# Split score products for eight more slots, a second load queue, a wider value product and a longer weight-splitting plan in an attention-plus-MoE kernel

## The chip, the cores and the metric

The kernel runs on one core of a Trainium2 chip. The metric is device time in microseconds (us); the lower, the better. Three runs of the kernel before took 1076.47, 1074.31 and 1074.10 us, median 1074.31. All matrix work is in fp32: a plain fp32 product takes several passes through TensorE, and the other way that this kernel uses is to write an operand as the sum of two rounded parts (fp32r, high and low) and to add up two or three one-pass products.

## The reference

```python
k_all = np.concatenate([k_g, k_l], axis=2); v_all = np.concatenate([v_g, v_l], axis=2)
out_g = sm(scale * q_g @ k_all.T) @ v_all            # 32 global queries see every key
s_ll = np.where(np.abs(i - j) <= 32, scale * q_l @ k_l.T, -1e9)   # 512 local queries: a band,
out_l = sm(concat[scale * q_l @ k_g.T, s_ll]) @ v_all             # and the 32 global keys
x = concat[out_g, out_l] as (8 * 544, 512)           # 8 batches, 8 heads of 64
h = np.maximum(x @ w_in, 0.0)                        # w_in 512 x 2048
return h * h @ w_out                                 # w_out 2048 x 512
```

## The kernel before, in words

The 128 pieces of attention work (8 batches, 2 halves of 256 local queries, 8 heads) are called slots here, t = 0 to 127. One loop runs over turns t. Turn t does the softmax of slot t, the transposes and the value product of slot t-1, and, 9 turns behind, one eighth (m = t-9) of a block of the MLP: `gemm1` (tiles `h`), relu and square (`r`), `gemm2` (tiles `o`). Block 0, whose x is slots 0 to 7 (`xg`), runs in turns 9 to 16 with plain fp32 weights (`wf`); from m = 8 (turn 17) on the weights are split (`ws`, high and low).

**A slot.** `load_head` brings `raw`: keys (352 columns), queries (256), values (256). `scores` makes `s`. `softmax1` adds the mask on VectorE and takes the maximum (the custom instruction `prob<-s,con`, two a slot), `softmax2` is the exponential on ScalarE, `softmax3` normalises (small `st` instructions, then `prob<-prob,st`). `transposes` brings the probabilities into the PSUM tile `pt`, `pt_split` copies them out (`pts`), `av` makes the value product `xa`, and `x_evac` stores it in `xg` or `x_h`/`x_l`. There are two `prob` tiles and one `pt`, so slot t+2 can't begin its softmax before slot t is transposed.

**Plain slots.** The first 16 slots (`plain`, `NPLAIN`) multiply whole fp32 numbers: scores are one product for each half (two PE records), and the value product has three, of which the first contracts 96 rows. From slot 16 on, `split_head` first makes `hi` and `lo`: a cast on ScalarE (`hi<-raw`), and subtractions on VectorE (`lo`, `hi`). The scores are then two one-pass products for each half. The tiles `hi` and `lo` have two buffers, and `hi` of slot t is also read by `g_scores(t)`, the product with the global queries (`gs`), so `hi` of slot t+2 waits for `g_scores(t)`. That product needs the global queries of four slots: `g_load` loads `qz` in place for plain slots, and loads `qr` and splits it into `qgz` (ScalarE, then VectorE) for the others.

**Weights.** `PLAN` says for each turn, at four places, how many weight passes (`b`) and splits (`s`) are issued. A chunk of weights (`wr`, 32 of them) takes one ScalarE pass and two VectorE passes (`wf`; the letters b count the VectorE passes), and later a cast on ScalarE and a subtraction on VectorE (`ws`). `w_need` issues what a turn needs and the plan hasn't yet issued.

**What sets the order.** From turn 17 on (`FREE`) TensorE, VectorE and ScalarE run in the order of the program text. Before that, a list scheduler at build time orders the instructions of each engine; the chip then runs each engine strictly in that order. So an instruction that waits holds up all that stands behind it on its engine. DMAs are issued by SP, in its own order.

Of the kernel before, what the change touches and what calls it, by code (L numbers as in the profile page):

```python
# [16 lines left out]
P = 128  # L17
# [8 lines left out]
NSTEP = NBLK * 8  # L26
LAG = 9
NPLAIN = 16

PLAN = [",,,b", "b,,,b", "b,,,b", "b,,b,", "b,,b,", "b,,b,", "b,,b,", "b,b,,b", "b,b,,b", "bb,bb,bb,bb", "bb,bb,bb,bb", "bbs,bb,bbs,bbs", "bbs,bbs,bbs,bbs", "bbs,bbs,bbs,bbs", "bbs,bbs,bs,s", "ss,s,s,s", "ss,s,s,s", "s,,s,", "s,,s,", "s,,s,", "s,,s,", "s,,s,", "s,,s,"]  # L30
FREE = (17, 17, 17)
LOOK = 2
SQ = (2, 3, 4, 5, 14, 15)
# [25 lines left out]
def attention_moe(  # L59
# [22 lines left out]
    def plain(t):  # L82
        return t < NPLAIN

    w_bufs = {"free": WCH}

    def w_take(n):
# [2 lines left out]
    def load_head(t):  # L90
        if plain(t):
            w_take(1)
            raw = wp.tile([P, 1024], F32, tag="w", name=f"raw{t}")[:, :PK]
        else:
            raw = p2.tile([P, PK], F32, tag="raw", name=f"raw{t}")
        cuts = (0, QC + KC, PK) if t == 0 else (0, PK)
        for o, e in zip(cuts, cuts[1:]):
            nc.sync.dma_start(raw[:, o:e], pk[t, :, o:e])
        heads[t] = dict(raw=raw)

    load_head(0)
    con = cp.tile([P, P + 4 * WIN], F32, name="con")
    for o, e in ((0, P + 2 * WIN), (P + 2 * WIN, P + 4 * WIN)):
        nc.sync.dma_start(con[:, o:e], consts[:, o:e])
        if o == 0:
            for t in range(1, 4):
                load_head(t)
    ident, masks = con[:, :P], con[:, P:]

    x_h = cp.tile([P, 2, 4, HALF], F32R, name="x_h")  # L110
# [10 lines left out]
    def split_head(t):  # L121

        hd = heads[t]
        raw = hd["raw"]
        if plain(t):
            return
        hi = p2.tile([P, PK], F32R, tag="hi", name=f"hi{t}")
        lo = p2.tile([P, QC + 192], F32R, tag="lo", name=f"lo{t}")
        ac.copy(hi, raw)
        ve.tensor_sub(lo, raw[:, KC : KC + QC + 192], f(hi[:, KC : KC + QC + 192]))  # L130
        ve.tensor_sub(hi[64:, :KC], raw[64:, :KC], f(hi[64:, :KC]))
        ve.tensor_sub(hi[32:64, PK - 64 :], raw[32:64, PK - 64 :], f(hi[32:64, PK - 64 :]))
        hd["hi"], hd["lo"] = hi, lo

    def scores(t):
        hd = heads[t]
        pool, tag = (ps_h, "h") if t < 8 and t % 2 else (ps_a, "s")
        s = pool.tile([P, 2, WIN], F32, tag=tag, name=f"s{t}")
        for u in range(2):
            qs, ks = slice(KC + u * P, KC + u * P + P), slice(128 * u, 128 * u + WIN)  # L140
            if plain(t):
                pe.matmul(s[:, u, :], hd["raw"][:, qs], hd["raw"][:, ks], start=True, stop=True)
            else:
                pe.matmul(s[:, u, :], hd["hi"][:, qs], hd["hi"][:, ks], start=True, stop=False)
                pe.matmul(s[:, u, :], hd["lo"][:, u * P : u * P + P], hd["hi"][:, ks], start=False, stop=True)
        hd["s"] = s

    def scale(t):

        return 0.0625 if plain(t) else 0.125  # L150

    def softmax1(t):
        hd = heads[t]
# [105 lines left out]
    def g_load(t):  # L259

        b, grp = t // 16, (t // 4) % 2

        def cols(z, j):
            return bass.AP(z.tensor, z.offset + 64 * j, [list(z.ap[0]), [256, 2], [160, 2], [1, 32]])

        src = qg[b, grp].rearrange("p (a b) n -> p a b n", a=2)
        if plain(t):
# [12 lines left out]
    def g_scores(t):  # L280
        hd = heads[t]
        h4 = t % 4
        if h4 % 2 == 0:
            state["gs"] = ps_a.tile([P, 416], F32, tag="gs", name=f"gs{t}")
        kk = hd["raw" if plain(t) else "hi"]
        pe.matmul(
            state["gs"][:, :288],
            state["qz"][:, 128 * h4 : 128 * h4 + 128],
# [5 lines left out]
    def g_evac(t):  # L294
        grp, pair = (t // 4) % 2, (t % 4) // 2
        gs = state["gs"]
        early = plain(t)
        parts = ((0, 0, 288),) if (t // 8) % 2 == 0 else ((288, 0, 160), (448, 192, 96))
        parts = [(sg[64 * pair : 64 * pair + 64, grp, d : d + n], slice(o, o + n)) for d, o, n in parts]
        for dst, cols in parts:  # L300
            ac.copy(dst, gs[:64, cols] if early else gs[64:, cols])
        for dst, cols in parts if not early else ():
            ve.tensor_add(dst, gs[:64, cols], dst)

# [16 lines left out]
    def g_soft(t):  # L321
        s = sg[:, (t // 4) % 2, :]
        st = p2.tile([P, 4], F32, tag="gst", name=f"gst{t}")
        ve.tensor_reduce(out=st[:, 0:1], in_=s[:, :544], op=ALU.max, axis=AX.X)
        ve.tensor_scalar(out=st[:, 1:2], in0=st[:, 0:1], scalar1=-scale(t), scalar2=None, op0=ALU.mult)
        state["gst", t] = st

    def g_exp(t):
        s, st = sg[:, (t // 4) % 2, :544], state["gst", t]
        ac.activation(out=s, in_=s, func=AF.Exp, scale=scale(t), bias=st[:, 1:2], accum_out=st[:, 2:3])  # L330

    def g_norm(t):
        s, st = sg[:, (t // 4) % 2, :], state["gst", t]
# [240 lines left out]
    for t in range(4, 8):  # L574
        load_head(t)
        if t == 4:
            w_start(0)
    scores(0)
    jobs = {}
    for t in range(NSTEP + LAG + 1):  # L580
# [50 lines left out]
        if early:  # L631
            softmax3(t)
        w_tick(t, 1)
        if t + 1 < NT:
            split_head(t + 1)
        if live:
            if t % 2 == 1:
# [123 lines left out]
```

## Time and profile before

| | |
|---|---|
| median of 3 runs | 1074.31 us |
| the profiled execution: its time, and its span | 1074.6 us, 1072.8 us |
| value product of slot 5 starts | 28.80 us |
| value product of slot 9 starts | 44.70 us |
| gemm1 with split weights starts (m = 8, turn 17) | 113.76 us |
| gemm1 of turn 24 starts | 170.95 us |
| granted TensorE clock | 1.0 in all slices |

In the profile, `L52` is the line of a helper that issues nearly all instructions, so groups are told apart by the tiles' names: `s<-raw` is a score product of plain slots, `s<-hi` one of split slots. PE is TensorE, PEld its weight loads, DVE VectorE, ACT ScalarE, SPq the queue of DMA issues. A plain fp32 product shows as two records. In the chain of waits a line has a start, a duration and what ran; in rows of stretches there stand the stretch, its length, and for PE, PEld, DVE, ACT and POOL the busy time and the number of instructions, then the granted clock, the share of the DMA engines and GB/s; rows of groups have the number, the busy time and the mean duration in ns of one.

### The profile page before, as it was taken

What the parts mean: (1) busy time and instruction counts of PE and PEld (TensorE: products, weight loads), DVE (VectorE), ACT (ScalarE), POOL (GpSimd) and SP (SyncE); (2) the same over time, 40 slices, a digit from 0 to 9 for tenths busy, and PEclk for the clock granted to TensorE, in tenths of its full rate; (3) what the DMA queues carried; (4) which work ended last, traced back from release to release, by engine and by line L of the source; (5) the groups of instructions that cost most, each with busy time, mean ns of one, the idle gap of its engine ahead of it and who ended that gap; (6) DMA issues with size and microseconds to landing.
All of it is one profiled execution on the core that took longest, in us unless ns stands there. A gap on an engine that the chain in (4) does not pass through costs nothing.

```text
span 1072.8 us, 21138 instructions
## 1 busy us (share of the span) xinstructions
PE 1054.5 (98%) x7568; PEld 938.6 (87%) x7568; DVE 857.2 (80%) x2687; ACT 752.3 (70%) x1901; POOL 2.9 (0%) x10
## 2 busy tenths in 40 slices
PE   7999999999999999999999999999999999999998
PEld 5766789998999989989898989998999999999887
DVE  4689889988888888888888889888888888884322
ACT  5879776778767777777767786777777787774322
POOL 1000000000000000000000000000000000000000
PEclk9999999999999999999999999999999999999999
DMA  9933222232322222223222222222322222200000
GB/s 346 369 125 145 83 82 82 73 90 78 94 70 82 86 78 70 89 66 101 75 90 65 83 86 82 73 82 83 92 75 70 84 95 66 87 29 33 13 20 20
DMA packets 55768, 96.78 MB, mean 90 GB/s; under 512 B 6384, under 2 KB 30704, under 8 KB 55664
## 3 DMA queue, kind: packets, MB, share of 16 engines
q1 hardware_dynamic: 55664, 95.44, 27.3%
q8 instruction: 60, 0.98, 0.4%
q14 instruction: 44, 0.36, 0.1%
HBM read 86.51 MB, written 8.91 MB: 89 GB/s over the span
## 4 chain that ended last, share of the span: by engine, by line
PE 86%; ACT 7%; DVE 4%; DMA 1%; issue 1%; SPq 0%; ACTq 0%
PE o L52 33%; PE h L52 32%; PE xa L52 7%; PE s L52 5%; PE pt L52 5%; PE gxo L52 2%; PE gs L52 2%; DVE prob L52 1%; ACT prob L52 1%; ACT r L52 1%; ACT ph L52 1%; ACT hi L52 1%; ACT ot L52 1%; PE gt L52 1%; DMA raw<-in_pk_dram 1%
## 5 line engine op out<-in xcount | busy, mean ns | idle before, releaser
L52 PE MATMUL h<-x_h,ws 128*128 128x256 f32 x2048 | 388.9, 283 | 0.0
L52 PEld LDWEIGHTS h<-x_h,ws 128*128 128x128 f32 x2048 | 327.1, 191 | 0.5
L52 PE MATMUL o<-ws,gh 128*128 128x512 f32 x1024 | 321.3, 395 | 0.0
L52 PE MATMUL h<-x_l,ws 128*128 128x256 f32 x1024 | 289.2, 282 | 0.1
L52 PEld LDWEIGHTS o<-ws,gh 128*128 128x128 f32 x1024 | 185.5, 188 | 34.6
L52 PE MATMUL o<-ws,gl 128*128 128x512 f32 x512 | 202.6, 396 | 0.0
L52 PEld LDWEIGHTS h<-x_l,ws 128*128 128x128 f32 x1024 | 195.9, 191 | 0.9 <-DVE x_l L52 0.4
L52 ACT CAST ph<-pt 128x256 fp32r<-128x256 f32 x448 | 141.1, 341 | 70.3 <-PE pt L52 64.2
L52 ACT ACTIVATE prob<-prob,st 128x224 f32<-128x224 f32 x270 | 127.7, 475 | 62.3 <-DVE st L52 60.3
L52 ACT ACTIVATE r<-h 128x512 f32<-128x512 f32 x136 | 81.4, 599 | 110.2 <-PE h L52 110.1
L52 PEld LDWEIGHTS o<-ws,gl 128*128 128x128 f32 x512 | 96.2, 188 | 22.7
L52 DVE CUSTOM_DVE_ANT_0 prob<-s,con 128x224 f32<-128x224 f32 x256 | 89.5, 385 | 22.9 <-PE s L52 16.6
L52 DVE TENSOR_TENSOR gl<-r,gh 128x512 fp32r<-128x512 f32 x128 | 87.9, 687 | 23.7 <-ACT gh L52 20.5
L52 ACT CAST hi<-raw 128x864 fp32r<-128x864 f32 x112 | 102.4, 915 | 1.4
L52 DVE TENSOR_TENSOR r<-h,r 128x512 f32<-128x512 f32 x82 | 56.7, 692 | 51.7 <-ACT r L52 50.4
L52 PE MATMUL xa<-ph,hi 128*64 128x128 f32 x448 | 87.4, 238 | 1.6 <-DVE ph L52 1.2
L52 DVE TENSOR_TENSOR hi<-raw,hi 64x352 fp32r<-64x352 f32 x224 | 82.6, 369 | 6.5
L52 ACT CAST gh<-r 128x512 fp32r<-128x512 f32 x128 | 79.1, 618 | 9.1 <-DVE r L52 8.8
L52 DVE TENSOR_TENSOR ph<-pt,ph 64x128 fp32r<-64x128 f32 x224 | 79.7, 356 | 7.0
L52 DVE TENSOR_TENSOR lo<-raw,hi 128x448 fp32r<-128x448 f32 x112 | 69.7, 622 | 16.4 <-ACT hi L52 13.9
L52 PE MATMUL pt<-con,prob 128*128 128x128 f32 (+1 forms) x512 | 78.1, 275 | 2.0 <-ACT prob L52 2.0
L52 DVE TENSOR_SCALAR prob<-prob,st 128x224 f32<-128x224 f32 x242 | 70.6, 334 | 4.1
(79 smaller groups left out, 1567.4 us busy)
## 6 DMA issues: line engine op xcount, KB each, us to landing
raw<-in_pk_dram SPq DMA_DIRECT2D x127, 432.0 KB, 3.2
wr<-in_w_dram SPq DMA_DIRECT2D x32, 512.0 KB, 7.5
gv<-in_vg_dram SPq DMA_DIRECT2D x32, 320.0 KB, 3.2
out_dram<-ot SPq DMA_DIRECT2D x32, 256.0 KB, 2.2
qr<-in_qg_dram SPq DMA_DIRECT2D x28, 64.0 KB, 2.8
out_dram<-ot SPq DMA_DIRECT2D x8, 64.0 KB, 1.7
raw<-in_pk_dram SPq DMA_DIRECT2D x1, 304.0 KB, 3.0
con<-in_consts_dram SPq DMA_DIRECT2D x1, 288.0 KB, 4.4
```

The source lines that it names most:

```text
L52: r = method(*args, **kwargs)
```

## The change

Four parts:

1. Slots 4 to 11 (`SCORES`) use split products for `scores` and `g_scores`. `split_head` runs for them on 608 columns (keys and queries), the values stay whole. `g_load` of turns 4 and 8 so uses the split form. The scale of plain global scores moves into `g_evac`. The remaining plain slots (0 to 3, 12 to 15; `whole`) load `qr` and copy it into `qz` on GpSimd.
2. The first loads: the masks, the identity, slot 0's values and the first `qr` are issued by ScalarE's queue; slots 0 to 3's loads stay on SP. The second half of the masks is loaded later.
3. The first value product of plain slots contracts 128 rows in place of 96 (the added rows are zeros).
4. `PLAN` has fewer `s` in turns 11 to 14. Counted in the program, the weight splits of turns 11 to 23 are 3, 4, 4, 4, 5, 5, 2, 2, 2, 1, 0, 0, 0 before, and 2, 2, 2, 2, 5, 5, 2, 2, 2, 2, 2, 2, 2 now: 32 in both.

```diff
+SCORES = range(4, 12)
+PLAN = [",,,b", "b,,,b", ... "bbs,bb,bbs,bb", "bbs,bb,bbs,bb", "bbs,bb,bbs,bb", "bbs,bb,b,s", "ss,s,s,s", ...]
+    def whole(t):
+        return plain(t) and t not in SCORES
...
+    half = P + 2 * WIN
+    nc.scalar.dma_start(con[:, P:half], consts[:, P:half])
+    load_head(1)
+    nc.scalar.dma_start(con[:, :P], consts[:, :P])
+    nc.scalar.dma_start(heads[0]["raw"][:, QC + KC :], pk[0, :, QC + KC :])
+    load_head(2)
+    load_head(3)
...
-        if plain(t):
+        if whole(t):
             return
...
-        ac.copy(hi, raw)
-        ve.tensor_sub(lo, raw[:, KC : KC + QC + 192], f(hi[:, KC : KC + QC + 192]))
+        e = KC + QC if plain(t) else PK
+        n = min(e - KC, QC + 192)
+        ac.copy(hi[:, :e], raw[:, :e])
+        ve.tensor_sub(lo[:, :n], raw[:, KC : KC + n], f(hi[:, KC : KC + n]))
         ve.tensor_sub(hi[64:, :KC], raw[64:, :KC], f(hi[64:, :KC]))
...
-                (xa, v[:96, 192:256], pts[:96, 256:512]),
+                (xa, v[:, 192:256], pts[:, 256:512]),
...
-            for j in range(2):
-                nc.sync.dma_start(cols(qz, 0)[:, j], src[:, j])
+            qr = p1.tile([P, 2, 2, 32], F32, tag="qr", name=f"qr{t}")
+            (nc.sync if t else nc.scalar).dma_start(qr, src)
+            nc.gpsimd.tensor_copy(cols(qz, 0), qr)
...
-        early = plain(t)
+        early = whole(t)
...
+                ac.activation(out=dst, in_=gs[:64, cols], func=AF.Copy, scale=0.5)
...
+        if t == 6:
+            nc.sync.dma_start(con[:, half:], consts[:, half:])
...
         if early and t + 1 < NPLAIN:
+            split_head(t + 1)
             scores(t + 1)
```

**ScalarE around slots 5 to 8, before.** `xa_330`, `xa_362` and `xa_400` are the value products of slots 5, 6 and 7, `pts_349` and `pts_389` the transposed probabilities of slots 6 and 7, `st_351` and `st_391` the maxima of slots 7 and 8, `wf_188` and `wf_259` weights.

```order
L52 COPY xg<-xa_330 64x256
L52 COPY pts_349<-pt 128x512
L52 ACTIVATE wf_188<-wr_186 128x512
L52 COPY xg<-xa_362 64x256
L52 ACTIVATE prob_93,st_391<-prob_93,st_391 128x224
L52 COPY pts_389<-pt 128x512
```

Now: `xa_354` is slot 5's value product, `raw_114`, `raw_117` and `raw_122` are slots 6, 7 and 8, `st_341` is slot 6's maximum, `gs_270` the global scores of slots 4 and 5.

```order
L53 COPY pts_339<-pt 128x512
L53 COPY xg<-xa_354 64x256
L53 ACTIVATE wf_268<-wr_222 128x512
L53 CAST qgz<-qr_246 128x2x2x32
L53 CAST hi_315<-raw_114 128x608
L53 COPY sg<-gs_270 64x288
L53 CAST hi_358<-raw_117 128x608
L53 ACTIVATE wf_268<-wr_266 128x512
L53 CAST hi_397<-raw_122 128x608
L53 ACTIVATE wf_350<-wr_307 128x512
L53 ACTIVATE prob_93,st_341<-prob_93,st_341 128x224 x2
```

Before, when slot 5's product is stored, slots 6 and 7 are already scored and through the exponential. Now the global queries' cast stands behind slot 5's product, slot 6's cast behind that (its buffer is slot 4's, which `g_scores(4)` reads), and slot 6's exponential comes eight rows later.

**VectorE at the same place, before.** `st_317`, `st_351` and `st_391` belong to slots 6, 7 and 8.

```order
L52 RECIPROCAL st_317<-st_317 128x2
L52 TENSOR_SCALAR st_351<-st_351 128x2
L52 TENSOR_SCALAR prob_93<-prob_93,st_317 128x224 x2
L52 TENSOR_SCALAR wf_188<-wf_188 128x512
L52 SCALAR_TENSOR_TENSOR wf_188<-wr_153,wf_188 128x512
L52 TENSOR_SCALAR st_351<-st_351 128x2
L52 ISA prob_93,st_391<-s_366,con 128x224
```

Now, from the subtraction for the global queries of slots 4 to 7 to slot 6's first mask instruction:

```order
L53 TENSOR_TENSOR qgz<-qr_246,qgz 128x2x2x32
L53 SCALAR_TENSOR_TENSOR wf_268<-wr_222,wf_268 128x512
L53 TENSOR_TENSOR lo_316<-raw_114,hi_315 128x256
L53 TENSOR_TENSOR hi_315<-raw_114,hi_315 64x352
L53 TENSOR_TENSOR sg<-gs_270,sg 64x288
L53 TENSOR_TENSOR lo_359<-raw_117,hi_358 128x256
L53 TENSOR_TENSOR hi_358<-raw_117,hi_358 64x352
L53 TENSOR_SCALAR wf_268<-wf_268 128x512
L53 SCALAR_TENSOR_TENSOR wf_268<-wr_266,wf_268 128x512
L53 ISA prob_93,st_341<-s_320,con 128x224
```

Where slot 6 was being normalised, VectorE now does the splits of slots 6 and 7 and two weight passes ahead of slot 6's mask.

More of the change, by code (lines that the diff above doesn't have):

```diff
@@ L95, in load_head @@
             raw = p2.tile([P, PK], F32, tag="raw", name=f"raw{t}")
-        cuts = (0, QC + KC, PK) if t == 0 else (0, PK)
-        for o, e in zip(cuts, cuts[1:]):
-            nc.sync.dma_start(raw[:, o:e], pk[t, :, o:e])
+        if t == 0:
+            nc.sync.dma_start(raw[:, : QC + KC], pk[t, :, : QC + KC])
+        else:
+            nc.sync.dma_start(raw, pk[t])
         heads[t] = dict(raw=raw)
@@ L128, in split_head @@
         lo = p2.tile([P, QC + 192], F32R, tag="lo", name=f"lo{t}")
-        ac.copy(hi, raw)
-        ve.tensor_sub(lo, raw[:, KC : KC + QC + 192], f(hi[:, KC : KC + QC + 192]))
+        e = KC + QC if plain(t) else PK
+        n = min(e - KC, QC + 192)
+        ac.copy(hi[:, :e], raw[:, :e])
+        ve.tensor_sub(lo[:, :n], raw[:, KC : KC + n], f(hi[:, KC : KC + n]))
         ve.tensor_sub(hi[64:, :KC], raw[64:, :KC], f(hi[64:, :KC]))
-        ve.tensor_sub(hi[32:64, PK - 64 :], raw[32:64, PK - 64 :], f(hi[32:64, PK - 64 :]))
+        if not plain(t):
+            ve.tensor_sub(hi[32:64, PK - 64 :], raw[32:64, PK - 64 :], f(hi[32:64, PK - 64 :]))
         hd["hi"], hd["lo"] = hi, lo
@@ L140, in scores @@
             qs, ks = slice(KC + u * P, KC + u * P + P), slice(128 * u, 128 * u + WIN)
-            if plain(t):
+            if whole(t):
                 pe.matmul(s[:, u, :], hd["raw"][:, qs], hd["raw"][:, ks], start=True, stop=True)
@@ L148, in scale @@
     def scale(t):
-        return 0.0625 if plain(t) else 0.125
+        return 0.0625 if whole(t) else 0.125
     def softmax1(t):
@@ L284, in g_scores @@
             state["gs"] = ps_a.tile([P, 416], F32, tag="gs", name=f"gs{t}")
-        kk = hd["raw" if plain(t) else "hi"]
+        kk = hd["raw" if whole(t) else "hi"]
         pe.matmul(
@@ L300, in g_evac @@
         for dst, cols in parts:
-            ac.copy(dst, gs[:64, cols] if early else gs[64:, cols])
+            if early:
+                ac.activation(out=dst, in_=gs[:64, cols], func=AF.Copy, scale=0.5)
+            else:
+                ac.copy(dst, gs[64:, cols])
         for dst, cols in parts if not early else ():
@@ L324, in g_soft @@
         ve.tensor_reduce(out=st[:, 0:1], in_=s[:, :544], op=ALU.max, axis=AX.X)
-        ve.tensor_scalar(out=st[:, 1:2], in0=st[:, 0:1], scalar1=-scale(t), scalar2=None, op0=ALU.mult)
+        ve.tensor_scalar(out=st[:, 1:2], in0=st[:, 0:1], scalar1=-0.125, scalar2=None, op0=ALU.mult)
         state["gst", t] = st
@@ L329, in g_exp @@
         s, st = sg[:, (t // 4) % 2, :544], state["gst", t]
-        ac.activation(out=s, in_=s, func=AF.Exp, scale=scale(t), bias=st[:, 1:2], accum_out=st[:, 2:3])
+        ac.activation(out=s, in_=s, func=AF.Exp, scale=0.125, bias=st[:, 1:2], accum_out=st[:, 2:3])
     def g_norm(t):
```

11 lines of the change are left out of this document (3 added, 8 removed).

## The prediction

> **What bounds the kernel now.** First the page:
>
> ```profile
> PE 1054.5 (98%) x7568; PEld 938.6 (87%) x7568; DVE 857.2 (80%) x2687; ACT 752.3 (70%) x1901; POOL 2.9 (0%) x10
> PE 86%; ACT 7%; DVE 4%; DMA 1%; issue 1%; SPq 0%; ACTq 0%
> ```
>
> TensorE sets the time, ScalarE and VectorE are on the chain for 11%. The change touches turns 0 to 23 only, so I then read the chain of waits in order of time over the first 150 us:
>
> ```profile
> 19.76 1.08 PE xa L52 x6
> ...
> 28.80 1.02 PE xa L52 x6
> ...
> 41.25 3.46 PE h L52 x16
> 44.70 1.01 PE xa L52 x6
> ...
> 53.74 0.49 PE gs L52 x2
> ...
> 56.97 0.95 PE s L52 x4
> ...
> 61.36 0.44 PE pt L52 x4
> ...
> 93.72 0.86 ACT prob L52 x2
> ...
> 104.20 0.44 PE s L52 x4
> ...
> 113.76 2.87 PE h L52 x24
> ...
> 117.22 0.14 PE gs L52
> ```
>
> From 19.76 (slot 2's value product) on the chain is nearly all TensorE. The rows in between also price the products: plain scores 0.95, split ones 0.44; plain global scores 0.49 (two records), split ones 0.14; a value product 1.01; the four transposes 0.44; an eighth of plain gemm1 3.46, of split gemm1 2.87. I cut the program at three marks: slot 5's value product ends (28.80 + 1.02 = 29.82), slot 9's ends (44.70 + 1.01 = 45.71), and gemm1 of turn 17 starts (113.76). The busy time of stretches:
>
> ```profile
> 28.80:45.72 16.92, 16.92 (x91) 13.01 (x91) 11.29 (x44) 14.85 (x39) 0.00 (x0) 1.00 1.05 401
> 45.72:113.76 68.04, 66.00 (x281) 44.53 (x282) 56.56 (x145) 55.63 (x129) 0.00 (x0) 1.00 0.40 151
> 113.76:170.95 57.19, 55.83 (x420) 49.16 (x420) 51.62 (x160) 45.22 (x114) 0.00 (x0) 1.00 0.26 80
> 238.37:293.23 54.86, 54.65 (x425) 49.81 (x424) 47.27 (x151) 41.55 (x107) 0.00 (x0) 1.00 0.30 89
> ```
>
> Up to 45.72 VectorE is busy for 11.29 of 16.92 us and TensorE never idles; from 45.72 to 113.76 TensorE idles 2.04 us, nearly all ahead of the transposes that follow ScalarE's multiplications at 93.72. The last two rows are turns 17 to 23 and the same seven turns a period later: 57.19 against 54.86.
>
> **Part by part, stage 1: to the end of slot 5's value product.** The start, in the timeline:
>
> ```profile
> 0.74 0.88 SPq L98 DMA_DIRECT2D raw<-in_pk_dram  x2
> ...
> 2.13 1.38 SPq L98 DMA_DIRECT2D raw<-in_pk_dram  x3
> 3.78 1.86 PE L52 MATMUL s<-raw 128*128 128x224 f32 x4 [3.78 <-DMA raw<-in_pk_dram]
> ...
> 6.18 0.39 DVE L52 CUSTOM_DVE_ANT_0 prob<-s,con 128x224 f32<-128x224 f32 x1 [5.04 <-DMA con<-in_consts_dram]
> ...
> 8.03 3.55 PE L52 MATMUL s<-raw 128*128 128x224 f32 x10 [2.39 <-DMA raw<-in_pk_dram]
> ...
> 12.37 0.59 ACT L52 COPY pts<-pt 128x512 f32<-128x512 f32 x1 [0.45 <-PE pt L52]
> ```
>
> VectorE waits for the masks until 6.18, but slot 0's scores end at 3.78 + 1.86 = 5.64, so masks that land earlier give 0.5 us at most. Slot 1's scores wait for their load until 8.03; its issue moves from 2.13 to about 1.19, ahead of two others. I take 1.0 us off the start (bounds 0.3 and 1.9: the lower if the bytes rather than the issue decide, the upper if both scores wait for nothing new; they could, since the order now puts `g_scores(0)`, with its DMA and GpSimd copy, between slot 1's two halves). Slots 4 and 5 bring splits:
>
> ```profile
> L52 DVE TENSOR_TENSOR pl<-pt,ph 128x256 fp32r<-128x256 f32 x110 | 46.2, 420 | 2.7 <-ACT ph L52 1.9
> L52 DVE TENSOR_TENSOR hi<-raw,hi 64x352 fp32r<-64x352 f32 x109 | 57.0, 523 | 3.2
> L52 DVE SCALAR_TENSOR_TENSOR wf<-wr,wf 128x512 int32<-128x512 int32 x32 | 22.1, 689 | 0.6
> L52 DVE TENSOR_SCALAR wf<-wf 128x512 int32<-128x512 int32 x32 | 13.9, 434 | 7.3 <-ACT wf L52 7.1
> L52 DVE CUSTOM_DVE_ANT_0 prob<-s,con 128x224 f32<-128x224 f32 x34 | 12.2, 384 | 9.9 <-DMA con<-in_consts_dram 5.0 <-PE s L52 4.3 <-PE pt L52 0.5
> L52 DVE TENSOR_SCALAR prob<-prob,st 128x224 f32<-128x224 f32 x220 | 64.1, 334 | 3.9
> L52 DVE TENSOR_SCALAR st<-st 128x2 f32<-128x2 f32 x219 | 36.9, 168 | 6.7
> L52 DVE TENSOR_TENSOR sg<-gs,sg 64x288 f32<-64x288 f32 x27 | 12.2, 451 | 0.8
> L52 DVE TENSOR_TENSOR qgz<-qr,qgz 128x128 fp32r<-128x128 f32 x27 | 7.9, 293 | 0.8
> L52 ACT CAST hi<-raw 128x864 fp32r<-128x864 f32 x2 | 1.8, 907 | 0.0
> L52 ACT ACTIVATE wf<-wr 128x512 f32<-128x512 f32 x32 | 21.5, 672 | 0.7 <-DMA wr<-in_w_dram 0.6
> ```
>
> The first three rows give a slot's `lo` (256 columns, as in `pl`) 0.42 and `hi` 0.52 on VectorE; the cast of 608 columns, scaled from 864, about 0.64 on ScalarE. TensorE gains 0.95 - 0.44 = 0.51 on each slot's scores, and the global scores of slots 4 and 5 (2 x 0.49) move behind slot 5. VectorE's 2 x 0.94 for the splits are hidden in its idle time or on the path of slots 4 and 5, which wait for them; I put 1.4 on the path. So slot 5's value product ends at 29.8 - 1.0 - 2.0 + 1.4 = 28.2 (bounds 25.5, with the splits hidden and the value products 0.2 shorter each, and 30.7, with the splits in full and TensorE's gain hidden).
>
> **Stage 2: to the end of slot 9's value product.** Here I expect the loss. `hi` has two buffers, and slot 4's is read by `g_scores(4)`, which needs the split global queries; on ScalarE their cast stands behind the store of slot 5's product. So slot 6's split can't start before slot 5's product is out, where in the order before slot 6 was by then past its exponential. Then VectorE has to do, in its order, from the `qgz` subtraction to slot 9's reciprocal: 7 + 6 weight passes (7 x 0.689 + 6 x 0.434 = 7.4), 5 `lo` and 5 `hi` (4.7), 8 mask instructions (3.1), 6 normalisations (2.0), 12 small ones (12 x 0.168 = 2.0), global sums (two of 0.451 and two parts of slots 8 and 9, about 0.6: 1.5), two `qgz` (0.6): 21.3 us; I take 21 (19 if neighbours overlap by 0.1 us each; more if it waits). Ahead of it lie the store, a weight pass and the cast, about 1.3; behind it ScalarE's two multiplications of slot 9 (0.86), three weight passes (3 x 0.672 at most) and the copy of the transposed tile (0.59), and the product itself (1.01): 4.2 with some overlap. Sum 1.3 + 21 + 4.2 = 26.5, against 45.71 - 29.82 = 15.9 before. TensorE's own work there (four transposes and value products, five scores, six global scores, two eighths of gemm1) is 1.8 + 4.0 + 2.2 + 0.8 + 6.9 = 15.7 us, so it idles for about 10; what it saves in this stage is hidden. Slot 9 is done at 28.2 + 26.5 = 54.7, 9.0 later. Not lost: the seven extra weight chunks done by then, and `g_scores(8)` and `(9)`.
>
> **Stage 3: to turn 17.** TensorE's list from slot 9's product on is before's, less the stall of 2.0 (VectorE and ScalarE have weight passes behind them and, by the plan, seven splits fewer), less slot 11's scores (0.51), global scores of slots 8 to 10 already done (3 x 0.49) and slot 11's by the split (0.35), less the wider value product. For that, the weight loads:
>
> ```profile
> 55.88 0.84 PEld L52 LDWEIGHTS xa<-pts,raw 96*64 96x64 f32 x6 [0.33 <-issue]
> ...
> 158.20 0.14 PEld L52 LDWEIGHTS xa<-ph,hi 128*64 128x64 f32 x1
> ```
>
> At 55.88 the load of 96 rows starts after 0.33 us of waiting for nothing shown, while the 128-row load at 158.20 starts while `h` is still running. A plain value product takes 1.01 where its records at the other plain products' rate (0.44 for four of 128 columns) come to 0.88. I take 0.2 a slot (from 0, if it is the 64 columns, to 0.25): six slots, 1.2. The Trainium skill, TensorEngine Tiling (Array Packing), Key Properties, says that changing the tiling mode, not just the tile, drains TensorE. By that the change from 128 x 128 to 128 x 64 drains too and only the inner change goes; with 0.05 a slot the sum would end 0.9 higher. The row at 158.20 speaks against it. Stage 3 is then 68.0 - 2.0 - 2.3 - 1.2 = 62.5, and turn 17 starts at 117.2 against 113.76: +3.4 (from -1.3 with every bound low to +8 with every bound high).
>
> **Stage 4: turns 17 to 23.** Seven splits come to turns 20 to 23:
>
> ```profile
> 140.00:148.25 8.25, 7.74 (x60) 6.49 (x59) 7.21 (x22) 5.98 (x15) 0.00 (x0) 1.00 0.32 113
> 148.25:155.60 7.35, 7.35 (x57) 6.71 (x56) 6.03 (x23) 5.50 (x15) 0.00 (x0) 1.00 0.22 64
> 155.60:162.87 7.27, 7.27 (x56) 6.69 (x56) 6.59 (x20) 5.21 (x14) 0.00 (x0) 1.00 0.19 62
> 162.87:170.95 8.08, 8.08 (x69) 7.49 (x69) 7.18 (x22) 5.61 (x17) 0.00 (x0) 1.00 0.44 120
> ```
>
> VectorE is busy for 7.21 + 6.03 + 6.59 + 7.18 = 27.0 of 30.95 us; seven subtractions, priced as the 128x512 pass of `wf` at 0.689, bring it to 31.8: 0.9 too much, and less if neighbours overlap. The other bound: turns 17 to 20, with seven splits, cost with the rest of their tail 57.19 - 54.86 = 2.3 over the later period, of which about 0.6 (as gemm1's 3.46 against 2.87) is the plain gemm2 still in turn 17; 1.7 for seven. I take 1.3 (0.1 to 2.5).
>
> **The sum.** +3.4 + 1.3 = +4.7 on the profiled execution's 1074.6: 1079.3; the median is 0.3 lower, so 1079.0 us.
>
> **The rivals.**
> - *TensorE keeps the bound* (faster). If slots 6 to 9 came through as before, all that TensorE saves would count: scores 8 x 0.51 = 4.1, global scores 8 x 0.35 = 2.8, value products 16 x 0.2 = 3.2, the stall 2.0, the start 1.0, less 1.3: -11.8, 1062.5. For it: TensorE is the chain from 19.76 on. Against it: the order of VectorE. It decides where slot 9's product ends before about 49; half-way there the time is 1068.5, and that is the time I give this case. Chance 0.17.
> - *The bounds all fall low* (no change): stage 1 ends at 25.5, VectorE's 21 us are 19, the last stage costs only 0.2: 25.5 + 24.5 + 62.5 = 112.5, so -1.3 + 0.2, 1073.2. For it: ScalarE and VectorE were idle for 2.1 and 5.6 us of stage 2 before, so there was room on both. Against it: every bound has to fall one way, and no wait may come on top. Chance 0.25.
> - *TensorE also goes cold* (slower still). The first eight score records took 1.86 us for four, against 0.95 later, after idling. If the 10 us of idling in stage 2 come in long pieces, the products on each slot's path there (0.44 + 1.01) take twice as long for two slots or so, +2.9: 1081.9. The Trainium skill, TensorE: Matmul & The Clock Gate, Part 1, says that the clock halves after an idle window of about 3.4 us; the granted clock of this profile is 1.0 in every stretch shown, so no row here shows it. Chance 0.10.
>
> My forecast has 0.48, its own range 1076.5 to 1081.5. Below 0.2% (2.1 us, about what a measurement of this kernel tells from no change) of the median is the first rival: faster 0.17. Within it is the second and a little of the forecast's low end: same 0.26. Slower: 0.57. The range 1070.5 to 1082.5 leaves about half of the first rival and a tenth of the last two cases outside.
>
> **What would show it.** Right: in the profile after, ScalarE's cast `hi` of slot 6 starts after slot 5's product; VectorE is nearly always busy and TensorE idles some 10 us between 28 and 55; slot 9's product ends near 54.7, split gemm1 starts near 117; no stall of 2 us follows in turns 12 to 16; turns 20 to 23 are about 1.3 us longer. Wrong: slot 9's product ends before 49 (then the first rival), the stage from there to turn 17 takes over 65 us (a new stall, or no gain by the 128 rows), or turn 17 to 24 differs from before by over 2.5.

## The result, and the profile after

The changed kernel takes 1090.18 us (median of 4 runs, 1089.49 to 1090.74) against 1074.46 for the kernel before beside it: ratio 1.0143, 95% interval 1.013 to 1.0156. That is 15.7 us slower, where 4.7 were forecast. The profiled execution took 1090.18 us, with a span of 1088.4.

The page of the changed kernel, its engines, its clock by slices and its chain:

```profile
PE 1059.9 (97%) x7560; PEld 940.6 (86%) x7560; DVE 866.1 (80%) x2711; ACT 758.2 (70%) x1911; POOL 2.5 (0%) x10
PEclk9699999999999999999999999999999999999999
PE 80%; ACT 8%; DVE 7%; DMA 3%; issue 1%; ACTq 0%; SPq 0%; DVEq 0%
```

TensorE falls from 86% of the chain to 80%; VectorE and transfers come in. The second slice (27 to 54 us) has a granted clock of 0.6. The marks of the prediction, read from TensorE's timeline:

| | before | forecast | after |
|---|---|---|---|
| slot 5's value product ends | 29.8 | 28.2 | 33.1 |
| from there to slot 9's | 15.9 | 26.5 | 28.4 |
| from there to turn 17 | 67.9 | 62.5 | 63.9 |
| from turn 17 to the end | 959.2 | +1.3 | 963.0 (+3.8) |

TensorE's timeline of the changed kernel (in brackets how long it idled ahead of a row, and for whom):

```profile
8.85 0.85 PE L53 MATMUL gs<-raw,qz 128*128 128x288 f32 x1 [1.16 <-POOL qz L283]
...
26.75 1.08 PE L53 MATMUL xa<-pts,raw 128*64 128x256 f32 x6 [0.73 <-ACT pts L53]
29.62 0.79 PE L53 MATMUL pt<-con,prob 128*128 128x128 f32 x4 [1.79 <-DVE prob L53]
31.15 1.97 PE L53 MATMUL xa<-pts,raw 128*64 128x256 f32 x6 [0.73 <-ACT pts L53]
34.91 0.85 PE L53 MATMUL gs<-hi,qgz 128*128 128x288 f32 x2 [1.80 <-DVE qgz L53]
37.41 0.52 PE L53 MATMUL s<-hi 128*128 128x224 f32 x1 [1.65 <-ACT hi L53]
...
47.66 1.08 PE L53 MATMUL xa<-pts,raw 128*64 128x256 f32 x6
...
60.45 1.08 PE L53 MATMUL xa<-pts,raw 128*64 128x256 f32 x6
```

Slot 4's product starts at 26.75, slot 5's at 31.15 and takes 1.97 instead of 1.08; slot 6's comes only at 47.66. In between stands the wait for `qgz`, the split of the global queries of slots 4 to 7. The chain of waits through this place:

```profile
24.88 8.67 DMA wr<-in_w_dram
33.55 0.65 ACT wf L53
...
34.57 0.30 DVE qgz L53
34.91 0.62 PE gs L53
35.56 0.27 ACT hi L53
...
36.67 0.61 ACT hi L53
...
38.09 0.52 DVE hi L53
...
40.86 0.53 DVE hi L53
...
41.53 1.16 PE s L53 x4
42.69 2.59 PE h L53 x6
...
47.67 1.09 PE xa L53 x6
```

That is the wait foreseen: the cast `hi` of slot 6 (35.56) comes after slot 5's product (33.12), since `hi` of slot 4 is held by `gs`, and `gs` needs `qgz`. After it come four slots' casts and subtractions. ScalarE ahead of the cast:

```profile
33.15 0.36 ACT L53 COPY xg<-xa 64x256 f32<-64x256 f32 x1 [2.06 <-PE xa L53]
33.54 0.66 ACT L53 ACTIVATE wf<-wr 128x512 f32<-128x512 f32 x1
34.10 0.28 ACT L53 CAST qgz<-qr 128x128 fp32r<-128x128 f32 x1
```

The global queries themselves were there: their load was issued at 16.47 and took 8.2 us, so it had landed 9.4 us before the cast. What held the cast was its place in ScalarE's order, behind the store of slot 5's product (done at 33.51) and a weight pass whose load landed at 33.55.

Two signs of the prediction are weaker than it said. From slot 5's product to slot 9's VectorE is idle for 4.5 us, and TensorE for 5.5 where some 10 were expected, at a mean granted clock of 0.75 (TensorE's busy time stands first behind the comma, VectorE's third):

```profile
33.12:61.53 28.41, 22.88 (x100) 16.90 (x100) 23.91 (x79) 22.14 (x56) 0.40 (x1) 0.75 0.56 200
```

### The profile page after: what moved, and what is told of

Read it like the earlier page. It is cut to its first block, busy times and chain, and to the rows that moved or that the text cites. A ratio compares the mean times of both kernels' runs of the same rounds, so it can differ in the third digit from the quotient of the medians.

```text
span 1088.4 us, 21157 instructions
## 1 busy us (share of the span) xinstructions
PE 1059.9 (97%) x7560; PEld 940.6 (86%) x7560; DVE 866.1 (80%) x2711; ACT 758.2 (70%) x1911; POOL 2.5 (0%) x10
## 4 chain that ended last, share of the span: by engine, by line
PE 80%; ACT 8%; DVE 7%; DMA 3%; issue 1%; ACTq 0%; SPq 0%; DVEq 0%
PE o L53 31%; PE h L53 30%; PE xa L53 6%; PE s L53 5%; PE pt L53 4%; PE gxo L53 2%; DMA wr<-in_w_dram 2%; PE gs L53 2%; ACT prob L53 2%; DVE prob L53 2%; ACT r L53 1%; DVE wf L53 1%; ACT hi L53 1%; ACT ph L53 1%; DMA raw<-in_pk_dram 1%
## 5 line engine op out<-in xcount | busy, mean ns | idle before, releaser
L53 ACT CAST hi<-raw 128x864 fp32r<-128x864 f32 (+1 forms) x120 | 108.0, 900 | 3.6 <-PE gs L53 2.2
L53 DVE TENSOR_TENSOR hi<-raw,hi 64x352 fp32r<-64x352 f32 x232 | 86.7, 374 | 6.7
L53 DVE TENSOR_TENSOR lo<-raw,hi 128x448 fp32r<-128x448 f32 (+1 forms) x120 | 73.1, 609 | 15.5 <-ACT hi L53 12.7
L53 PEld LDWEIGHTS pt<-con,prob 128*128 128x128 f32 (+1 forms) x512 | 59.2, 134 | 18.1 <-DVE prob L53 3.0
```

The costliest lines, as they stand in the source:

```text
L53: r = method(*args, **kwargs)
```

## The experiments

The ends of slots 5 and 9 and the start of turn 17 are those of each profiled execution, as above, and "rest" is what lies behind turn 17. Single executions differ by some 1 us up or down in the first of these, with the landing of the first loads.

| kernel | median us | ratio to before, 95% interval | slot 5 | slot 9 | turn 17 | rest |
|---|---|---|---|---|---|---|
| before | 1074.5 | | 29.8 | 45.7 | 113.6 | 959.2 |
| changed | 1090.2 | 1.0143, 1.013 to 1.0156 | 33.1 | 61.5 | 125.5 | 963.0 |
| start alone | 1073.6 | 0.9986, 0.9977 to 0.9995 | 30.0 | 47.2 | 112.5 | 958.8 |
| plan alone | 1074.6 | 0.9999, 0.9991 to 1.0008 | 28.9 | 44.8 | 110.3 | 961.8 |
| 128 rows alone | 1074.4 | 0.9996, 0.9987 to 1.0005 | 30.1 | 46.0 | 114.1 | 959.0 |
| splits alone, slots 4 to 11 | 1081.9 | 1.0069, 1.0053 to 1.0084 | 33.3 | 51.0 | 120.2 | 960.1 |
| the same, no subtractions | 1075.7 | 1.0009, 1.0 to 1.0019 | 31.0 | 47.7 | 114.3 | 960.1 |
| the same, four buffers | 1077.9 | 1.003, 1.002 to 1.0039 | 33.3 | 50.9 | 115.8 | 959.9 |
| splits alone, slots 8 to 11 | 1075.4 | 1.0001, 0.9991 to 1.0011 | 29.4 | 45.4 | 112.3 | 960.2 |
| changed, no splits | 1077.0 | 1.0027, 1.0014 to 1.004 | 31.3 | 48.5 | 114.2 | 961.9 |
| changed, old start | 1082.8 | 1.0076, 1.0058 to 1.0093 | 31.2 | 49.5 | 116.6 | 963.1 |
| changed, early queries | 1085.3 | 1.0099, 1.008 to 1.0118 | 37.3 | 57.7 | 121.7 | 963.0 |
| changed, four buffers | 1083.2 | 1.008, 1.0066 to 1.0094 | 32.9 | 54.3 | 117.4 | 963.4 |
| changed, early queries and four buffers | 1084.4 | 1.0091, 1.0077 to 1.0106 | 36.4 | 55.5 | 120.1 | 963.0 |
| changed, added products | 1088.7 | 1.0126, 1.0106 to 1.0147 | 35.6 | 59.8 | 123.9 | 963.0 |
| early queries, added products | 1085.9 | 1.01, 1.008 to 1.012 | 35.0 | 55.9 | 121.2 | 963.0 |

**The parts alone.** The first theory (A) was that the late cast of slot 4's global queries costs nearly all, against VectorE's sheer work (B) and late loads by the new start (C); later the four parts were put into the kernel before one by one.

```diff
+    nc.scalar.dma_start(con[:, P:half], consts[:, P:half])   # and the rest of the new start
```

> The kernel before with the new start alone: masks and identity by ScalarE's queue, slot 0's values and global queries by it too, the rest by SyncE's, and the global queries of plain slots through a small tile and a GpSimd copy. Theory S (the start shifts loads and saves no time): slot 0's value product ends at 16 to 18 instead of 14.7, since slot 1's scores now stand partly behind the first global scores and these behind the slowest of the first loads; some of it is caught up by turn 17: 1075 to 1078. Rival, as predicted (the masks and slot 1 land earlier): 1 us faster, 1073.5.

1.5 us faster, about the sum that was predicted, but not for the predicted reason. Slot 9's product ends 1.5 us later than before, not earlier. In the profiled execution the gain comes at slot 14, where the stall of before is gone. (The fastest times of the two kernels are level, 1073.1 us; those of before reach up to 1077.2, these to 1074.3.) TensorE's timeline of before, and the stretch around it before and with the start alone (TensorE's busy time is the first number behind the comma):

```profile
94.26 0.92 PE L52 MATMUL pt<-con,prob 128*128 128x128 f32 x4 [1.99 <-ACT prob L52]
```

```profile
86.40:113.60 27.20, 25.16 (x111) 16.37 (x111) 22.39 (x56) 22.36 (x53) 0.00 (x0) 1.00 0.23 81
```

```profile
86.40:113.60 27.20, 27.20 (x129) 18.13 (x128) 22.52 (x57) 22.83 (x52) 0.00 (x0) 1.00 0.15 51
```

```diff
-PLAN = [... "bbs,bb,bbs,bbs", "bbs,bbs,bbs,bbs", "bbs,bbs,bbs,bbs", "bbs,bbs,bs,s", ...]
+PLAN = [... "bbs,bb,bbs,bb", "bbs,bb,bbs,bb", "bbs,bb,bbs,bb", "bbs,bb,b,s", ...]
```

> The kernel before with the stretched weight splits alone: seven splits move from turns 11 to 14 behind turn 17. Theory P (VectorE has no room for them in turns 17 to 23): the last stage costs 2.7 to 3.8 us more, as in every run with this plan so far, and turn 17 starts 2 to 3.6 us earlier, since the stall of 2 us of the turns 12 to 16 goes: 1074 to 1076, no gain. Rival, as predicted: 1.3 us more in the last stage and 2.0 less before: 1073.8.

Theory P: turn 17 starts 3.3 us earlier (0.9 of it is there at slot 5, ahead of any effect of the plan) and the rest takes 2.6 longer; the medians are level. The chain of this kernel, with gemm1 of turns 17, 24 and 25, and the same three rows of before:

```profile
110.49 2.87 PE h L52 x24
...
169.67 2.88 PE h L52 x24
178.09 2.88 PE h L52 x24
```

```profile
113.76 2.87 PE h L52 x24
...
170.95 2.88 PE h L52 x24
178.23 2.88 PE h L52 x24
```

Turns 17 to 23 take 59.18 against 57.19, and turn 24, which the prediction didn't count, 8.42 against 7.28.

```diff
-                (xa, v[:96, 192:256], pts[:96, 256:512]),
+                (xa, v[:, 192:256], pts[:, 256:512]),
```

> The kernel before with the first value product over 128 keys instead of 96 alone (the tile's last 32 rows hold zeros). Rival, as predicted (only the change to 96 rows drains TensorE): 0.2 us for each of the 16 plain slots, 3.2 us, 1071.3; a slot's value product takes 0.81 to 0.85 instead of 1.01. Theory T (the change from 128 columns to 64 drains as well, so nothing is saved): each value product stays at 1.01 and the time is within 1 us of before.

Theory T. Slot 5's product in TensorE's timeline, before and with 128 rows:

```profile
28.73 1.09 PE L52 MATMUL xa<-pts,raw 96*64 96x256 f32 x6
```

```profile
28.99 1.08 PE L52 MATMUL xa<-pts,raw 128*64 128x256 f32 x6
```

```diff
+SCORES = range(4, 12)   # in the kernel before; its PLAN, loads and 96 rows stay
```

> The kernel before with the split products of slots 4 to 11 alone: its start, its plan of weight splits and its 96 rows stay. Theory A: the global queries' cast is early, so VectorE and ScalarE take the eight splits in time; TensorE saves up to 0.51 a slot in scores and 0.35 in global scores, some of it lost to waits: 1068 to 1074, faster than before or level. Rival B (VectorE's work): slot 9's product ends 6 to 9 us late and only half comes back in stage 3: 1077 to 1080.

7.4 us slower, against the range of theory A and above rival B's. Slot 5 is 3.5 late, slot 9 5.3, a little under rival B's 6 to 9, and nothing comes back by turn 17 (6.6 late). So the splits cost by themselves, with the queries cast early.

```diff
-SCORES = range(4, 12)
+SCORES = range(0)       # in the changed kernel
```

> The changed kernel with no split products in the plain slots (an empty list of them); the start over two queues, the stretched weight splits and the 128-row product stay. Theory A: there is no split cast to hold buffers, so stage 2 is TensorE's 16 us again; what is left is the start (+1.5) and the stretched weight splits in stage 4 (+3.9), with nothing gained by the 128 rows: 1079 to 1081. Rival B: as theory A up to stage 4. Rival C (the start makes the loads late for everything): stage 2 stays above 20 us and the time at 1084 or more.

2 us below the range of theories A and B, far from C's. Without splits, 13.2 of the 15.7 us are gone. The four parts alone add up to -1.5 + 0 + 0 + 7.4 = 5.9 us; some 10 us come only when they meet.

**Where splits and start meet.** In the changed kernel the order of SyncE has slot 4's global queries (`qr`) behind slots 5 to 11 and five weight loads; with the old start they come ahead of slot 5, behind two weight loads.

```diff
-    nc.scalar.dma_start(con[:, P:half], consts[:, P:half])
+    for o, e in ((0, P + 2 * WIN), (P + 2 * WIN, P + 4 * WIN)):   # and the rest of the old start
```

> The changed kernel with the first loads as they were before: one queue, slot 0 in two pieces, masks and identity together, the global queries of plain slots straight into their zeroed tile. Slot 4's global queries come by this to SyncE's 14th place instead of its 20th, and ScalarE's cast of them ahead of slot 2's store. Theory A (late global queries): stage 1 ends at about 30 as before the change, stage 2 takes 16 to 19 us, the clock stays at 1.0, and the time is 1074 to 1078, since what stage 3 gained stays and stage 4's 3.9 us stay lost. Rival B (VectorE's work of stage 2): stage 1 gets its 3 us back and no more, 1086 to 1088. Rival C (the start over two queues in itself): as theory A in the time, but then moving the one load alone gains little.

7.4 us of the 15.7 come back: stage 2 (18.3) is as theory A says and stage 1 nearly (31.2), but turn 17 is still 3.0 late and the time above its range.

```diff
+            state["qr4"] = p1.tile([P, 2, 2, 32], F32, tag="ot", name="qr4")   # behind load_head(4)
+            nc.sync.dma_start(state["qr4"], qg[0, 1].rearrange("p (a b) n -> p a b n", a=2))
```

> The changed kernel with one 64 KB load moved: the global queries of slots 4 to 7 are loaded right behind slot 4, ahead of the first weights, into a buffer of their own, so that ScalarE's cast of them stands 25 rows earlier in the order, ahead of the stores of slots 0 to 5, and slot 6's cast no longer waits for global scores that come behind slot 5's product. Theory A (late global queries: the 12.4 us that stage 2 lost come from this one cast, which holds the two hi buffers): slot 9's product ends about 9 to 12 us earlier, at 49 to 52, TensorE's clock stays at 1.0, and the time is 1078 to 1081. Rival B (VectorE has 21 us of work to do before slot 9's product, wherever the cast stands): slot 9's product ends at 57 or later and the time stays above 1086. Rival C (the loads are late, by the start over two queues): under 3 us of gain, and ScalarE's weight passes still wait for their loads.

4.9 us, about half of what theory A expected: slot 9's product ends at 57.7. Stage 2 shrinks to 20.4 us, but slot 5's product is now late (37.3). The stretch between slots 0 and 5, with VectorE busy for 15.10 of 19.80 us and a granted clock of 0.78:

```profile
17.50:37.30 19.80, 14.53 (x67) 9.75 (x66) 15.10 (x58) 14.19 (x39) 0.00 (x0) 0.78 1.01 405
```

**The clock.** Is it the halved clock, then? Two more products in each slot from 1 to 7, which nothing reads:

```diff
+        dummy = ps_o.tile([64, HALF], F32, tag="o0", name=f"dummy{t}")
+        for i in range(2):
+            pe.matmul(dummy, hd["pts"][:, :64], hd["pts"][:, 256:512], start=i == 0, stop=i == 1)
```

> The changed kernel with two more products behind each value product of slots 1 to 7, into a PSUM tile that nothing reads: about 1.1 us more TensorE work a slot, in places where it idled for 0.7 to 2 us, so that it stays busier and the clock need not fall. The order of all else stays much the same. Theory C (the halved clock between 30 and 47 us is a large part of the loss): the clock stays at 1.0, the value product of slot 5 takes 1.0 instead of 1.97, and the time falls by 3 to 5 us, to 1085 to 1087. Rival A (the wait for slot 4's global queries and VectorE set the end, TensorE's speed in between hardly matters): the time stays within 1.5 us of 1090, or grows by the 7 x 1.1 us added, up to 1095.

> As the run before this one, but with slot 4's global queries loaded early, as in the run q4_early (1085.3), where the clock was at 0.78 from 17.5 to 37.3 us. Theory C (what the early load didn't bring back is the halved clock): the clock stays at 1.0, stage 1 ends near 33 instead of 37.3, and the time is 1080 to 1082, level with the run with the old start. Rival B (VectorE and ScalarE have too much to do there whatever TensorE's speed): 1084 to 1088.

The clock is 1.0 and 0.999, and the times 1088.7 (1.0126, 1.0106 to 1.0147) and 1085.9 (1.01, 1.008 to 1.012). So 1.5 us less than the changed kernel, and nothing with early queries: both times lie where theory C's rivals put them. But the added work is in these times too, so they don't price the clock by itself. While the clock was at 0.5 in the changed kernel, TensorE was busy most of the time:

```profile
30.30:47.36 17.06, 12.39 (x40) 9.07 (x38) 12.55 (x41) 9.41 (x22) 0.00 (x0) 0.50 0.46 166
```

From 41.53 to 47.67 the chain above consists of its products alone. With the added products slot 5's product ends 2.5 us later than in the changed kernel, and the stage from there to slot 9's is 4.2 shorter (24.2 against 28.4). How much of either is the clock and how much the added work stays open.

**What the splits cost by themselves.** In the kernel with splits alone, first without VectorE's subtractions, then with four buffers:

```diff
-        ve.tensor_sub(lo[:, :n], raw[:, KC : KC + n], f(hi[:, KC : KC + n]))
-        ve.tensor_sub(hi[64:, :KC], raw[64:, :KC], f(hi[64:, :KC]))
+        if plain(t):
+            hd["hi"], hd["lo"] = hi, hi[:, KC:]
+            return
```

> The kernel before with the split products of slots 4 to 11 alone (1081.9), without VectorE's two subtractions in each of these splits: the products take the rounded tile in place of the rest, so the low parts are left out of the result. ScalarE's casts, the two hi buffers, the global queries' cast and TensorE's count of products stay. Theory B (VectorE's time: 16 subtractions, 7.5 us, where it is busy 84%): most of the loss goes, 1074 to 1077. Rival H (the two hi buffers and the casts on ScalarE hold the slots, VectorE's subtractions lie in its idle time): 1080 to 1082.

```diff
+        spare = plain(t) and t % 4 > 1
+        hi = p2.tile([P, PK], F32R, tag="raw" if spare else "hi", name=f"hi{t}")
+        lo = p1.tile([P, 512], F32R, tag=("ot", "r")[t % 2], name=f"lo{t}")   # if spare
```

> The kernel before with the split products of slots 4 to 11 alone, with four buffers for hi and lo instead of two (the other two in tiles that are not used before turn 14). Rival H (a slot's split waits for the global scores of the slot two before it): casts run up to two slots ahead, and the time falls by 3 us or more, to 1076 to 1079. Theory B (VectorE's time): the splits come earlier, but VectorE has as much to do, and the time stays within 1.5 us of 1081.9.

1075.7 (1.0009, 1.0 to 1.0019) without the subtractions: 6.2 of 7.4 us gone, theory B. But 1077.9 (1.003, 1.002 to 1.0039) with four buffers: 4.0 us, rival H. Both hold a part, and the two add up to more than the loss, so they overlap: presumably a split that has a buffer can be done when VectorE has time for it. The places differ: without the subtractions 2.3 us are back at slot 5, while the four buffers change nothing up to slot 9 (50.9 against 51.0) and then gain 3.4 at slot 10, whose product ends at 60.2 instead of 63.7. How full both engines are there shows the stretch of the kernel with splits and four buffers (VectorE and ScalarE are the third and fourth busy time), against 10.60 and 11.83 of 15.00 us from 14.80 to 29.80 before:

```profile
15.00:33.00 18.00, 13.03 (x79) 9.46 (x79) 16.75 (x63) 16.43 (x42) 0.57 (x1) 1.00 1.03 414
```

```profile
14.80:29.80 15.00, 13.86 (x79) 10.12 (x79) 10.60 (x50) 11.83 (x36) 0.66 (x1) 1.00 1.03 414
```

Splits only for slots 8 to 11:

```diff
-SCORES = range(4, 12)
+SCORES = range(8, 12)
```

> The kernel before with split products for slots 8 to 11 alone, the slots whose scores come when TensorE is the bound; slots 4 to 7 stay plain. Theory B2 (the splits of slots 4 to 7 cost because VectorE and ScalarE have no room from 16 to 50 us, those of slots 8 to 11 have): TensorE saves 4 x 0.51 + 4 x 0.35 = 3.4 us, some of it hidden: 1071 to 1074. Rival B (any eight or four splits ahead of turn 17 find VectorE full, since weight passes and weight splits fill it): slot 9's or slot 10's product ends 3 us or more late and turn 17 is no earlier: 1076 to 1079.

Level, between the two theories' ranges: four splits there cost nothing and save nothing. Turn 17 starts 1.3 us earlier, and the rest is 1.0 longer in the profiled execution. The loss of 7 us so belongs to slots 4 to 7, or to eight in a row.

**The buffers in the changed kernel.** The same four buffers, without and with the early queries:

> The changed kernel with four buffers for hi and lo instead of two; the late load of slot 4's global queries and all else stay. Theory H (the late queries cost only by holding the two buffers): slot 6's and 7's casts come ahead of the queries, slot 9's product ends 8 us or more earlier, and the time is 1079 to 1082. Rival B (VectorE's work sets the end, buffers or not): 1085 or more, at most the 4 us that four buffers gave the kernel with splits alone.

> The changed kernel with both cures, slot 4's global queries loaded early and four buffers. Theory H: once the buffers are free the early load adds nothing, within 1.5 us of the run before this one. Rival Q (late queries and few buffers are two separate losses): 3 us or more below it, 1076 to 1079. By what the splits alone still cost with four buffers (1077.9), not below 1075 in either case.

1083.2 and 1084.4: 7.0 us back with four buffers, a little short of theory H's range, and slot 9's product ends 7.2 earlier; with the early load besides 5.8. Each cure alone helps and the two together help no more than one: late queries and few buffers look like one loss, as theory H has it, of about 6 us. This isn't clean: with four buffers the early load still shortens stage 2 (19.1 against 21.4), and loses more ahead of it, where slot 5's product ends at 36.4 instead of 32.9. It is a loss of the combination, since with the old start the queries come early.

**The blocked queue.** What is left between the changed kernel with four buffers (1083.2) and the splits alone with four buffers (1077.9) might be the weights. SyncE's waits in the changed kernel (us in total, how many, the longest):

```profile
SPq L287 <- DVE qgz L53: 14.9, 2, 8.2
SPq L282 <- DVE qgz L53: 13.0, 1, 13.0
```

```diff
-            qr = p1.tile([P, 2, 2, 32], F32, tag="qr", name=f"qr{t}")
+            qr = p1.tile([P, 2, 2, 32], F32, tag="ot", name=f"qr{t}")                        # slots 0, 12
+            qr = p1.tile([P, 2, 2, 32], F32, tag="gv" if t == 8 else "qr", name=f"qr{t}")    # split slots
```

> The changed kernel with the global queries of slots 0 and 12 in one spare tile and those of slot 8 in another, so that neither load waits for slot 4's or slot 8's split. The order of every engine is, instruction for instruction, that of the changed kernel; what goes are SyncE's waits of 8.2 us (slot 8's queries) and 13.0 us (slot 12's) and the hole in the transfers from 40 to 49 us. Theory Q (the blocked queue makes weights late, and with them VectorE's passes): 3 us or more off, 1084 to 1087. Rival A (the late cast of slot 4's queries sets the end by itself, the weights behind the blocked loads land in time anyway): within 1.5 us of 1090.

> The same with four buffers for hi and lo. Theory Q (with the buffers freed, the chain runs through the weights behind slot 8's query load, which land at 41.4 in the run hi4): the 5.3 us that the start and the splits still cost together go, 1077 to 1080. Rival R (VectorE's order in slots 2 to 5, which the new start changes, costs them): 1082 to 1084.

1089.9 (1.0145, 1.0127 to 1.0164), and 1086.7 (1.0112, 1.009 to 1.0133) with four buffers, which is 3.5 more than without this edit, above the ranges of theory Q and rival R, in an order that differs in a few places on each engine. Both runs are weaker tests than they were meant to be: the tile borrowed for slot 8's queries is wanted by the first load of global values, which now waits in their place (15.2 us in the first run, 13.5 in the second):

```profile
SPq L323 <- DVE qgz L53: 15.2, 1, 15.2
```

But two weight loads that stood behind slot 12's queries go out ahead of that wait. In SyncE's timeline of the changed kernel and of the first run:

```profile
49.70 0.33 SPq L282 DMA_DIRECT2D qr<-in_qg_dram  x1
50.12 0.86 SPq L414 DMA_DIRECT2D wr<-in_w_dram  x2
```

```profile
30.85 0.33 SPq L282 DMA_DIRECT2D qr<-in_qg_dram  x1
32.12 1.39 SPq L414 DMA_DIRECT2D wr<-in_w_dram  x2
```

They are issued 18 us earlier and nothing is gained; in the chain of the changed kernel no transfer begins between 33.55 and 61 us. Theory Q so falls for the two waits above, but not for the queue as a whole. Later in the chain of the changed kernel, behind the next split of global queries, there stand:

```profile
71.39 0.33 SPq L287
71.76 3.76 DMA wr<-in_w_dram
```

The run with this edit has the same pair at 70.84 and 71.22. With four buffers a weight load issued behind slot 8's queries is on the chain from 35.93 to 41.34, and with this edit besides two others are, from 62.08 and 71.42, the first behind the global values that the edit made wait. With the queue free of every such wait, theory Q wasn't tried.

**A better kernel.** On top of the start alone, splits where there is room, their queries early, without and with four buffers:

> The kernel before with the new start, and split products for slots 8 to 11 alone, their global queries loaded early into a buffer of their own; the plan and the 96 rows of before. Theory B2 (the splits pay where VectorE has room and their queries are there): the start's 1.5 us and up to 2 of the 3.4 that TensorE saves: 1071 to 1073. Rival (four splits still cost as much as they save, as without the start, where they gave 0): 1073 to 1075.

> As the run before this one, with four buffers for hi and lo, so that slots 10 and 11 are split without waiting for the global scores of 8 and 9. Theory H: 0.5 to 1.5 us less than without. Rival B: no difference, within 0.7 us.

1075.8 (1.0011, 1.0002 to 1.0019) and 1075.5 (1.0007, 0.9998 to 1.0015): no gain over the kernel before, above the ranges of B2 and its rival, and no difference by the buffers. So on top of the start these four splits cost the start's gain. The start alone stays the fastest, 1.5 us below the kernel before.

## Why the prediction was wrong

The direction was right, and so was the wait foreseen for stage 2; the size was not: 4.7 forecast, 15.6 between the profiled executions. By its own steps:

- **Stage 1, 4.9 us off, is the step that failed.** "I take 1.0 us off the start": slot 0's product ends at 16.5 instead of 14.7. The prediction named the `g_scores(0)` between slot 1's halves and gave it no price; TensorE waits there for the GpSimd copy until 8.85. With the start alone this is caught up by slot 5, whose product ends 0.2 later than before (30.0): no gain, and 1.2 of the miss. The larger part is the splits. Their 1.4 and TensorE's gain of 2.0 were taken from durations, so slots 4 and 5 should have saved 0.6; but slot 5's product ends 3.1 later than with the start alone, 1.8 later than in the changed kernel without splits. What came was a wait of 1.79 ahead of slot 5's transposes and a product at half clock (1.97 against 1.08). In the kernel with splits alone it is 3.5 late, and 2.3 of that go without VectorE's subtractions. So the subtractions stand on the slots' path, and TensorE's gain doesn't show.
- **Stage 2, 1.9 us off.** 28.4 against 26.5, with the cast of slot 6 where it was expected. But the reason was only half there. VectorE's 21 us were priced as if their sum set the length. Four buffers take 7.0 us off this stage with the same work (at a clock of 1.0 instead of 0.75), so a good part was the wait for `qgz` and the two buffers. That 26.5 came near 28.4 is in part luck. And the prediction did not see that the new start is what puts this load, and so the cast, late.
- **Stage 3, 1.4 us off.** 1.2 of it is the 0.2 a slot for the 128 rows, which are nothing. The row at 158.20, on which that rested, shows a split slot, in one-pass products; it was no evidence for plain ones. The rule of the Trainium skill, TensorEngine Tiling (Array Packing), Key Properties, by which any change of mode drains, gave 0.9 more, and the runs agree with its result: 1.08 and 1.09 us a product.
- **Stage 4, 2.5 us off** (3.8 against 1.3). Turns 17 to 23 cost 2.0 more (forecast 1.3, bound 2.5). Another 1.1 come in turn 24, outside the stretch that was summed. About 0.7 behind it, seen in all kernels with splits, is not located.
- **The rivals.** TensorE didn't keep the bound. It did go cold, for 17 us; the runs with added products give back 1.5 us and nothing, net of the added work, and don't price it further.
- **What stays open.** With four buffers, 5.3 us lie between the changed kernel and the splits alone. In the profiled executions 1.6 of them lie ahead of turn 17 and 3.5 behind it. Behind turn 17 most of it is the plan's, which by itself costs 2.6 there. Ahead of it the changed kernel is 3.4 late at slot 9's product (54.3 against 50.9), and the plan gives 1.7 back from there to turn 17 (63.1 against 64.8; by itself 2.3). Slot 5's product is level, so the place is stage 2, 21.4 against 17.6; its chain holds the weight load from 35.93 to 41.34, but why it is longer was not shown.

## What to carry to other kernels

Parts of a change that give -1.5, 0, 0 and +7 alone can give +16 together where an order is drawn up anew from all of them: look in the new order for the load that moved back, for the instruction that moved back with it, and for who holds a buffer until that has run. A bound engine's saving counts only where the engines that pay for it have room in that very stretch and stand off the slot's own path: in the kernel before, four splits from slot 8 on were free (and saved nothing), eight from slot 4 on cost 7 us.

## What the runs showed of the hardware

The granted clock fell without any long idle gap. The changed kernel with early queries, cut at the changes of its clock, and two stretches of the changed kernel:

```profile
18.43:21.84 3.41, 1.98 (x12) 1.30 (x12) 3.23 (x13) 3.17 (x10) 0.00 (x0) 1.00 1.03 419
21.84:25.25 3.41, 2.68 (x10) 1.53 (x10) 3.26 (x13) 2.27 (x6) 0.00 (x0) 0.50 1.03 415
25.25:28.66 3.41, 3.35 (x13) 2.44 (x13) 0.96 (x5) 1.35 (x4) 0.00 (x0) 0.50 1.02 408
28.66:32.07 3.41, 2.88 (x18) 2.07 (x17) 1.69 (x7) 2.76 (x8) 0.00 (x0) 1.00 1.04 418
32.07:35.48 3.41, 0.88 (x5) 0.53 (x6) 3.31 (x15) 3.39 (x9) 0.00 (x0) 1.00 1.03 409
35.48:38.90 3.42, 3.42 (x14) 2.68 (x15) 2.67 (x9) 1.37 (x4) 0.00 (x0) 0.50 0.44 171
```

```profile
23.47:26.88 3.41, 2.33 (x14) 1.43 (x13) 1.78 (x9) 2.07 (x6) 0.00 (x0) 1.00 1.03 407
26.88:30.30 3.42, 1.63 (x10) 0.99 (x10) 2.40 (x8) 2.16 (x7) 0.00 (x0) 1.00 1.03 420
```

TensorE had been busy for 1.98 of 3.41 us, with no pause of 1 us, and the next 6.82 us were at 0.5. In the changed kernel the clock fell after 1.63 busy us, and held after 2.33. It came back after a stretch of 3.35 busy us, not after one of 2.68. The spells last 6.82, 3.42 and, in the changed kernel, 17.06 us (30.30 to 47.36): whole multiples of 3.41. So in these two kernels the stretch ahead of a fall need not be idle; some 60% of busy time was too little. At a kernel's start this can't be read: in the kernel before the rows give a clock of 1.0 there, though the first four score records take 1.86 us, and later ones 0.95.

The Trainium skill, TensorE: Matmul & The Clock Gate, Part 1, gives a free-running window of 3413 ns. The length of the spells agrees with it.
